# Values of late head pairs on 64 by 32 tiles of TensorE, and two score blocks moved to the other row half

## The chip, the cores and the metric

One Trainium2 chip, of which the kernel uses one core. The metric is device time in microseconds (us) of one launch; 1 us is 1000 ns. A difference under 0.2% (1.76 us) can't be told from no change here.

## What is computed

Sliding-window attention over 8 batches x 8 heads x 576 positions x 64 dims, plain in the first four heads and with dilation 4 in the others, and then a feed-forward layer on the concatenated heads:

```python
scores = q @ k.T / sqrt(64)           # 64 heads in all; a query sees the 32 keys up to its own
attn   = softmax(where(mask, scores, -1e9))
x      = (attn @ v) as 4608 tokens x 512
h      = x @ w_in                     # 512 -> 2048
g      = where(h >= 1, h, where(h <= -1, 0, (h + 1)**2 / 4))
out    = g @ w_out                    # 2048 -> 512
```

## The kernel before

**The feed-forward part** fills most of the time. It goes over 9 blocks of 512 tokens x 16 blocks of 128 hidden units, 144 steps. A step's `layer1` (L515) is 12 matmuls of 128x128 weights against 512 columns, `layer2` (L556) is 12 more, for the step two before. Activations and weights are split into a high and a low part, so each product is three matmuls.

**The attention** is laid between these steps. Heads go in 32 pairs `n`; of a pair, head j=0 has its queries and keys in partitions 0 to 63 and head j=1 in partitions 64 to 127 (the two *row halves* of TensorE). Dilated heads are stored by residue class, so every head is a band: a block of 32 queries needs 64 keys. There are 18 blocks `b` to a head.

Pairs 0 to 3 are early pairs with code of their own. For the others, the late pairs 4 to 31:

- `scores(n)` makes 36 matmuls (L227), one for each block and head: 64 contraction rows, 32 query columns as weights, 64 keys streamed. Each is on a 64 by 32 *tile* of TensorE, that is one row half and one of four column groups `g`; 8 tiles exist. `late_place` says which column group and which place `u` a block takes. Four rounds visit the 8 tiles in turn, and a fifth has the 4 matmuls left. Blocks 8 and 9 have u=4, the *rest* place: both heads share one 128x64 result there, j=0 in partitions 0 to 63, j=1 in 64 to 127.
- `masks` adds the mask table on VectorE (L266, L274, L281), the softmax runs on VectorE, ScalarE and GpSimd, `transpose` (L340) turns the probabilities into `pts`.
- `late_values(n)` makes 20 matmuls (L400) that add into the cleared tile `o`: five key blocks x two key halves (the row half) x two heads, 64 weight columns (the head dims), and 96, 64 or 32 queries streamed. They are on 64 by 64 tiles, of which there are 4. Key half 0 writes the first PSUM bank of `att`, half 1 the second.

`visit_step` (L588) does one attention *visit*: values of pair n, then scores of pair n+1, then the DMA issue of q and k for pair n+2. It runs between `layer1` and `layer2` of every fourth step, for n from 8 to 31; pair 31 has no scores after it. In a visit the j=0 scores go to a spare bank, j=1's to the second bank of `att`, and the rest place to the first bank of `att`. For pairs 4 to 7 a hand-written order (`FIRST`) has steps `V4`..`V7` and `S4`..`S8`, where values and scores stand apart, with feed-forward work between. There the two heads' rest results are in two banks, and `masks` takes two 64-partition operations for them (L281).

Every fp32 matmul shows in the trace as two *passes*: weight load, matmul, weight load, matmul. So 20 matmuls are 40 passes and 36 are 72. The matmuls of the feed-forward part have one pass each.

The order of all engines but the DMA completion is fixed by the order of the calls (a manual schedule).

Of the kernel before, what the change touches and what calls it, by code (L numbers as in the profile page):

```python
# [6 lines left out]
F32 = mybir.dt.float32  # L7
# [4 lines left out]
ALU = mybir.AluOpType  # L12
AX = mybir.AxisListType

B, H, S, D = 8, 8, 576, 64
DM, DF = 512, 2048
WIN, DIL = 32, 4
QB, NB = 32, S // 32
KW = 64
KPAD = S + 32  # L20
# [8 lines left out]
EARLY = 4  # L29
# [37 lines left out]
def body(ctx, tc, qk, v_early, v, mask, mask4, w_in, w_out, out):  # L67
    nc = tc.nc
# [3 lines left out]
    pool = ctx.enter_context(tc.tile_pool(name="pool", bufs=1))  # L72
# [8 lines left out]
    def bank(i, name):  # L81
        return ps.tile([128, TOK], F32, tag=f"b{i}", name=name)

    def banks_of(which, name):
        if which is None:
            both = ps.tile([128, 2, TOK], F32, tag="att", name=name)
            return both, [both[:, 0], both[:, 1]]
        return None, [bank(i, f"{name}_{i}") for i in which]
# [3 lines left out]
    heads, tables = {}, {}  # L92
# [21 lines left out]
    def load_qk(n):  # L114
        hd = heads.setdefault(n, {})
        if "qk" not in hd:
            hd["qk"] = pool.tile([128, 1216], F32, tag="qk", name=f"qk{n}")[:, :S + KPAD]
        hd["q"], hd["k"] = hd["qk"][:, :S], hd["qk"][:, S:]
        nc.sync.dma_start(out=hd["qk"], in_=qk[n])

    def load_v(n, queue=nc.sync):
        hd = heads.setdefault(n, {})
# [34 lines left out]
    def late_place(j, b):  # L157

        half, m, odd = b >= 10, b // 2, b % 2
        if half:  # L160
            return 3 - odd, 5 * j + m - 5
        if m < 4:
            return odd, 5 * j + m
        return (odd if j == 0 else 3 - odd), 4
# [36 lines left out]
                skip_group_check=True,  # L201
            )

    def scores(n, banks=None, at=None):
        if n < EARLY:
            return early_scores(n)
        hd = heads[n]
        cc = pool.tile([128, 704], F32, tag="c", name=f"c{n}", bufs=2)
        hd["cc"] = cc
        hd["c"] = cc[:, :576].rearrange("p (u x) -> p u x", x=KW)  # L210
        hd["st"] = cc[:, 576:603].rearrange("p (s u) -> p s u", s=3)
        if at is None:
            both, (one, two) = banks_of(banks, f"s{n}")
            hd["s"] = both, one[:, : 4 * KW], two[:, : 4 * KW], one[:, 4 * KW : 5 * KW], two[:, 4 * KW : 5 * KW]
        else:
            hd["s"] = None, *at
        todo = {}
        for j in range(2):
            for b in range(NB):
                todo.setdefault(late_place(j, b)[0] + 4 * j, []).append((j, b))  # L220
        for i in range(5):
            for tile in range(8):
                for j, b in todo[tile][i : i + 1]:
                    g, u = late_place(j, b)
                    src = hd["s"][1 + j] if u != 4 else hd["s"][3 + j]
                    r = slice(64 * j, 64 * j + 64)
                    PE.matmul(  # L227
                        out=src[QB * g : QB * g + QB, KW * (u % 5 % 4) : KW * (u % 5 % 4) + KW],
                        lhsT=hd["q"][r, QB * b : QB * b + QB],
                        rhs=hd["k"][r, QB * b : QB * b + KW],  # L230
                        start=True,
                        stop=True,
                    )
# [23 lines left out]
    def by_head(cc):  # L257

        return cc[:, : 10 * KW].rearrange("p (j x) -> p j x", j=2)

    def masks(n, only=None):
        both, *src = heads[n]["s"]
        c, m = heads[n]["c"], msk[:, n % 4 // 2]
        rest = m[:, : 4 * KW].rearrange("p (u x) -> p u x", x=KW)
        if both is not None:
            nc.vector.tensor_tensor(  # L266
                out=by_head(heads[n]["cc"])[:, :, : 4 * KW],
                in0=both[:, :, : 4 * KW],
                in1=m[:, : 4 * KW].unsqueeze(1).broadcast_to([128, 2, 4 * KW]),
                op=ALU.add,  # L270
            )
        for j in range(2) if both is None else ():
            if only in (None, j):
                nc.vector.tensor_tensor(  # L274
                    out=c[:, 5 * j : 5 * j + 4], in0=src[j].rearrange("p (u x) -> p u x", x=KW), in1=rest, op=ALU.add
                )
        if only in (None, 2):
            apart = src[2] is not src[3]
            for j in range(1 + apart):
                r = slice(64 * j, 64 * j + 64) if apart else slice(0, 128)  # L280
                nc.vector.tensor_tensor(out=c[r, 4], in0=src[2 + j][r], in1=m[r, 4 * KW :], op=ALU.add)  # L281

    def spread(n, s):
        st = heads[n]["st"]
# [104 lines left out]
        hd["o"] = list(pieces(n, both, ops))  # L389

    def late_values(n):
        hd = heads[n]
        att, at = hd.pop("at")
        for i in range(5):
            for half in range(2):
                m = 4 * half + i
                a, z = (64, 96) if (half, i) == (1, 0) else (0, 64 if i == 4 else 96)
                r = slice(64 * half, 64 * half + 64)
                for j in range(2):
                    PE.matmul(  # L400
                        out=at[64 * j : 64 * j + 64, 64 * m + a : 64 * m + z],
                        lhsT=hd["v"][r, j, i],
                        rhs=pts[r, 5 * j + i, a:z],
                        start=False,
                        stop=True,
                        skip_group_check=True,
                    )
        hd["o"] = list(joint_pieces(n, at))
        return att

    def joint_pieces(n, at):
        b, c = divmod(n, 4)
        tok0 = b * S
        end = TOK - tok0 % TOK
        step = 1 if c < 2 else DIL
        cuts = sorted({0, min(end, S), S})
        for a, z in zip(cuts, cuts[1:]):
            t, off = divmod(tok0 + a, TOK)
            src, here = at[:, a:z], slice(off, off + z - a)
            if step == 1:  # L420
                yield src, t, c, lambda x, here=here: x[:, here]
            else:
                src = at.rearrange("p (r i) -> p i r", r=DIL)[:, a // DIL : z // DIL]
                yield src, t, c, lambda x, here=here: x[:, here].rearrange("p (i r) -> p i r", r=DIL)
# [161 lines left out]


    def visit_step(s, n):  # L588
        att = late_values(n)
        if n + 1 < NP:  # L590
            spare = bank(4 + s % 2, f"s{n}")
            rest = att[:, 0, :KW]
            scores(n + 1, at=[spare[:, : 4 * KW], att[:, 1, 4 * KW :], rest, rest])
        if n + 2 < NP:
            load_qk(n + 2)
        if n + 1 < NP and n % 2:
            load_v(n + 1)
# [37 lines left out]
    def small_step(count):  # L635
# [14 lines left out]
            out=tables[int(i)], in_=mask4[:, 320 * int(i) : 320 + 384 * int(i)]  # L650
# [51 lines left out]
    for n in range(8, NP):  # L702
        s = 4 * (n - 4) - 2
# [113 lines left out]
```

## Time and profile before

| | |
|---|---|
| median of 3 runs | 878.5 us (878.21 to 878.94) |
| profiled execution | 879.35 us, of which the span is 877.5 us |
| TensorE busy | 869.2 us, 99% of the span |
| TensorE clock granted | full (0.999 on average) |
| VectorE, ScalarE, GpSimd busy | 63%, 35%, 13% |
| mean DMA rate | 66 GB/s |

The profile is one execution. Its timeline view merges neighbouring instructions of one group into a row. A TensorE matmul's shown length runs from when it is taken up to when its last result is written, so matmuls that follow one another overlap in it; the pace is read from the starts. Weight loads are a row of their own (PEld).

### The profile page before, as it was taken

To read this page: it belongs to the slowest core of one execution; us is meant where nothing else is said; L and a number is where in the kernel's file an instruction comes from. 1 tells how busy PE (TensorE), PEld (TensorE's weight loads), DVE (VectorE), ACT (ScalarE), POOL (GpSimd) and SP (SyncE) were. 2 spreads that over 40 slices of the span, in tenths; PEclk is the share of its full clock that TensorE was granted. 3 is DMA by queue.
4 is the path that set the end of the run, shared out by engine and by line. 5 is a ranking of instruction groups with operands and counts; after the bars stand their busy time and mean duration, and the time that the engine had idled before them with its cause. 6 is when DMAs were issued, how large, how long until landed. Compare 5 with 4: busy or idle time off the path is not lost.

```text
span 877.5 us, 16764 instructions
## 1 busy us (share of the span) xinstructions
PE 869.2 (99%) x7138; PEld 712.7 (81%) x7138; DVE 555.6 (63%) x1083; ACT 309.7 (35%) x520; POOL 109.7 (13%) x81
## 2 busy tenths in 40 slices
PE   9999999999999999999999999999999999999998
PEld 7777888888888888888888888888888888888886
DVE  6898887666766676666666666667666443334332
ACT  3988633233333333323323232323332222222222
POOL 2355531110010111111111011011111000000000
PEclk9999999999999999999999999999999999999999
DMA  9981012101210021101210121102110010001001
GB/s 353 415 330 58 30 58 77 60 28 59 76 58 30 4 92 40 59 28 59 78 58 29 59 77 45 36 7 86 50 58 2 1 49 1 0 1 49 1 0 49
DMA packets 17354, 58.12 MB, mean 66 GB/s; under 512 B 1920, under 2 KB 2432, under 8 KB 15232
## 3 DMA queue, kind: packets, MB, share of 16 engines
q1 hardware_dynamic: 17280, 57.06, 18.0%
q8 instruction: 56, 0.92, 0.4%
q14 instruction: 18, 0.15, 0.1%
HBM read 47.61 MB, written 9.44 MB: 65 GB/s over the span
## 4 chain that ended last, share of the span: by engine, by line
PE 92%; ACT 4%; DVE 4%; issue 1%; ACTq 0%; DVEq 0%
PE acc L556 42%; PE h L515 42%; PE o L400 3%; PE s L227 2%; DVE pts L340 1%; PE o L227 1%; DVE m_wi L486 1%; DVE h L535 1%; DVE gl L547 1%; PE s L244 0%; ACT m_wi L473 0%; ACT y L531 0%; PE fill L138 0%; DVE y L525 0%; ACT gh L542 0%
## 5 line engine op out<-in xcount | busy, mean ns | idle before, releaser
L556 PE MATMUL acc<-wo,gh 128*128 128x512 f32 x1152 | 381.8, 392 | 0.1
L515 PE MATMUL h<-xh,wi 128*128 128x512 f32 x1152 | 357.6, 390 | 0.6 <-DVE gl L547 0.5
L556 PEld LDWEIGHTS acc<-wo,gh 128*128 128x128 f32 x1152 | 216.4, 188 | 47.0 <-ACT gh L542 0.5
L515 PEld LDWEIGHTS h<-xh,wi 128*128 128x128 f32 x1152 | 216.2, 188 | 46.3 <-DVE gl L547 1.1
L531 ACT ACTIVATE y<-y,small 128x512 f32<-128x512 f32 x144 | 104.2, 723 | 367.0 <-DVE y L525 366.9
L556 PE MATMUL acc<-wo,gl 128*128 128x512 f32 x576 | 224.8, 390 | 0.3 <-DVE gl L547 0.2
L515 PE MATMUL h<-xl,wi 128*128 128x512 f32 x576 | 224.4, 390 | 0.0
L525 DVE TENSOR_SCALAR y<-h 128x512 f32<-128x512 f32 x144 | 99.4, 690 | 148.5 <-PE h L515 147.5
L535 DVE TENSOR_TENSOR h<-h,y 128x512 f32<-128x512 f32 x144 | 100.7, 700 | 77.5 <-ACT y L531 77.2
L547 DVE TENSOR_TENSOR gl<-h,gh 128x512 fp32r<-128x512 f32 x144 | 99.4, 691 | 69.4 <-ACT gh L542 69.3
L340 DVE STREAM_TRANSPOSE pts<-c 32x256 f32<-32x256 f32 (+2 forms) x336 | 123.1, 366 | 5.7
L556 PEld LDWEIGHTS acc<-wo,gl 128*128 128x128 f32 x576 | 108.2, 188 | 22.6 <-DVE gl L547 1.0
L515 PEld LDWEIGHTS h<-xl,wi 128*128 128x128 f32 x576 | 108.2, 188 | 22.3
L542 ACT CAST gh<-h 128x512 fp32r<-128x512 f32 x144 | 84.4, 586 | 106.8 <-DVE h L535 106.1
L299 POOL TENSOR_TENSOR c<-c 128x576 f32<-128x576 f32 x28 | 32.3, 1154 | 407.7 <-DVE c L291 407.6
L321 POOL TENSOR_TENSOR c<-c 128x576 f32<-128x576 f32 x30 | 35.5, 1183 | 109.4 <-DVE c L317 109.4
L303 ACT ACTIVATE c<-c 128x576 f32<-128x576 f32 x30 | 20.6, 685 | 74.4 <-POOL c L299 64.0
L400 PEld LDWEIGHTS o<-pts,v 64*64 64x64 f32 x1120 | 24.4, 133 | 10.1 <-issue 9.9
L400 PE MATMUL o<-pts,v 64*64 64x96 f32 (+2 forms) x1120 | 28.4, 241 | 0.1
L371 DVE TENSOR_TENSOR xl<-o,xh 128x128 fp32r<-128x128 f32 (+7 forms) x68 | 26.5, 431 | 2.1 <-ACT xh L367 2.1
L367 ACT CAST xh<-o 128x64 fp32r<-128x64 f32 (+9 forms) x68 | 23.3, 398 | 2.7 <-PE o L400 2.6
L227 PE MATMUL s<-qk 64*32 64x64 f32 x1096 | 23.1, 224 | 0.5 <-issue 0.5
(100 smaller groups left out, 369.4 us busy)
## 6 DMA issues: line engine op xcount, KB each, us to landing
qk<-qk_in SPq DMA_DIRECT2D x29, 592.0 KB, 4.0
v<-v_in SPq DMA_DIRECT2D x28, 320.0 KB, 4.5
raw_wi<-w_in SPq DMA_DIRECT2D x8, 1024.0 KB, 13.0
raw_wo<-w_in SPq DMA_DIRECT2D x8, 1024.0 KB, 14.7
out<-out SPq DMA_DIRECT2D x32, 256.0 KB, 2.4
wi_first<-qk_in SPq DMA_DIRECT2D x2, 592.0 KB, 7.7
wo_first<-v_early_in SPq DMA_DIRECT2D x2, 384.0 KB, 11.1
out<-outs SPq DMA_DIRECT2D x3, 256.0 KB, 2.0
```

The source lines that it names most:

```text
L227: PE.matmul(out=src[QB * g : QB * g + QB, KW * (u % 5 % 4) : KW * (u % 5 % 4) + KW], lhsT=hd["q"][r, QB * b : QB * b + QB], rhs=hd["k"][r, ...
L299: nc.gpsimd.tensor_tensor(out=c, in0=c, in1=spread(n, 0), op=ALU.subtract)
L321: engine.tensor_tensor(out=c, in0=c, in1=spread(n, 2), op=ALU.mult)
L340: nc.vector.transpose(out=to, in_=c)
L400: PE.matmul(out=at[64 * j : 64 * j + 64, 64 * m + a : 64 * m + z], lhsT=hd["v"][r, j, i], rhs=pts[r, 5 * j + i, a:z], start=False, stop=Tr ...
L515: PE.matmul(out=hp, lhsT=weight("wi", f, w, slice(128 * c, 128 * c + 128)), rhs=xtile(t)[x][:, c], start=start and (c, w, x) == terms[0], ...
L525: nc.vector.tensor_scalar(out=gs[t, f][0], in0=hps[t, f], scalar1=-1.0, scalar2=1.0, op0=ALU.max, op1=ALU.min)
L531: nc.scalar.activation(out=y, in_=y, func=AF.Square, bias=half_t, scale=0.5)
L535: nc.vector.tensor_tensor(out=hp, in0=hp, in1=gs[t, f][0], op=ALU.max)
L542: nc.scalar.copy(out=g_tile("gh", t, f), in_=hps[t, f])
L547: nc.vector.tensor_tensor(out=g_tile("gl", t, f), in0=hp, in1=gh.bitcast(F32), op=ALU.subtract)
L556: PE.matmul(out=acc[m], lhsT=g[:, 128 * m : 128 * m + 128], rhs=weight("wo", f, w, slice(0, DM)), start=f == 0 and i == 0, stop=f == NF - ...
```

## The change

It does three things. The values of a late pair are cut in their weight columns: each of the 20 matmuls with 64 head dims becomes two with 32 (`part` 0 to 3 instead of j 0 to 1), on the same 64 by 32 tiles as the scores. Of the scores, blocks 8 and 9 of head j=1 (u=4) take their queries and keys from partitions 0 to 63, from a second copy of these (`again`) that the host appends to q and k; so the rest place is written by one row half only. The load of q and k of a late pair is 1344 columns instead of 1184. Where the rest results were in two banks they are now in one, and `masks` needs one operation for them. `late_values` becomes a generator `value_rounds` that `late_values` runs to its end; `scores` has an argument `rounds` that no caller gives, so values still stand wholly ahead of scores.

```diff
     def load_qk(n):
...
-            hd["qk"] = pool.tile([128, 1216], F32, tag="qk", name=f"qk{n}")[:, :S + KPAD]
-        hd["q"], hd["k"] = hd["qk"][:, :S], hd["qk"][:, S:]
-        nc.sync.dma_start(out=hd["qk"], in_=qk[n])
+            hd["qk"] = pool.tile([128, 1344], F32, tag="qk", name=f"qk{n}")
+        w = S + KPAD + (160 if n >= EARLY else 0)
+        hd["q"], hd["k"], hd["again"] = hd["qk"][:, :S], hd["qk"][:, S:], hd["qk"][:, S + KPAD :]
+        nc.sync.dma_start(out=hd["qk"][:, :w], in_=qk[n][:, :w])
...
-    def scores(n, banks=None, at=None):
+    def scores(n, banks=None, at=None, rounds=None):
...
-                todo.setdefault(late_place(j, b)[0] + 4 * j, []).append((j, b))
+                g, u = late_place(j, b)
+                todo.setdefault(g if j == 0 or u == 4 else g + 4, []).append((j, b))
         for i in range(5):
+            if rounds is not None:
+                next(rounds, None)
             for tile in range(8):
                 for j, b in todo[tile][i : i + 1]:
                     g, u = late_place(j, b)
-                    src = hd["s"][1 + j] if u != 4 else hd["s"][3 + j]
-                    r = slice(64 * j, 64 * j + 64)
+                    if j and u == 4:
+                        r, at_q, at_k = slice(0, 64), hd["again"][:, QB * (b - 8) :], hd["again"][:, QB * (b - 6) :]
+                    else:
+                        r, at_q, at_k = slice(64 * j, 64 * j + 64), hd["q"][:, QB * b :], hd["k"][:, QB * b :]
+                    src = hd["s"][1 + j] if u != 4 else hd["s"][3]
...
         if only in (None, 2):
-            apart = src[2] is not src[3]
-            for j in range(1 + apart):
-                r = slice(64 * j, 64 * j + 64) if apart else slice(0, 128)
-                nc.vector.tensor_tensor(out=c[r, 4], in0=src[2 + j][r], in1=m[r, 4 * KW :], op=ALU.add)
+            nc.vector.tensor_tensor(out=c[:, 4], in0=src[2], in1=m[:, 4 * KW :], op=ALU.add)
...
     def late_values(n):
+        rounds = value_rounds(n)
+        for _ in rounds:
+            pass
+
+    def value_rounds(n):
...
-                for j in range(2):
+                for part in range(4):
+                    x = slice(QB * (part % 2), QB * (part % 2) + QB)
+                    j = part // 2
                     PE.matmul(
-                        out=at[64 * j : 64 * j + 64, 64 * m + a : 64 * m + z],
-                        lhsT=hd["v"][r, j, i],
+                        out=at[QB * part : QB * part + QB, 64 * m + a : 64 * m + z],
+                        lhsT=hd["v"][r, j, i, x],
                         rhs=pts[r, 5 * j + i, a:z],
...
+            yield
```

TensorE's order in a visit, before (a row is line, result tile, operands, partitions x columns of the result, count; `o` is the bank pair `att`, `s` the spare bank):

```order
L400 MATMUL o_1590<-pts,v_1525 64x96 [waits DVE_49,DMAHW4_49,PE_49,Activation_49]
L400 MATMUL o_1590<-pts,v_1525 64x96
L400 MATMUL o_1590<-pts,v_1525 64x32 [waits DVE_49]
L400 MATMUL o_1590<-pts,v_1525 64x32
L400 MATMUL o_1590<-pts,v_1525 64x96 x12
L400 MATMUL o_1590<-pts,v_1525 64x64 x4
L227 MATMUL s_1690<-qk_1528 32x64 [waits DMAHW6_49]
L227 MATMUL s_1690<-qk_1528 32x64 x3
```

The same place with the change:

```order
L412 MATMUL o_1665<-pts,v_1600 32x96 [waits DVE_49,DMAHW4_49,PE_49,Activation_49]
L412 MATMUL o_1665<-pts,v_1600 32x96 x3
L412 MATMUL o_1665<-pts,v_1600 32x32 [waits DVE_49]
L412 MATMUL o_1665<-pts,v_1600 32x32 x3
L412 MATMUL o_1665<-pts,v_1600 32x96 x24
L412 MATMUL o_1665<-pts,v_1600 32x64 x8
L234 MATMUL s_1785<-qk_1603 32x64 [waits DMAHW6_49]
L234 MATMUL s_1785<-qk_1603 32x64 x3
```

The counts of the values double, all on half the columns; the waits, and the scores' place behind the last value, stay.

VectorE's order around `mask4`, before (`s` is the score tile, `c` the masked scores):

```order
L266 TENSOR_TENSOR c_555<-s_556,small 128x2x256
L281 TENSOR_TENSOR c_555<-s_556,small 64x64 x2
```

The same place with the change:

```order
L273 TENSOR_TENSOR c_555<-s_556,small 128x2x256
L285 TENSOR_TENSOR c_555<-s_556,small 128x64
```

One operation less, here and in `mask5` to `mask8`.

## Rows read from the trace of the kernel before

**Rows 1.** The page: busy share of each engine, and the chain that ended last.

```profile
PE 869.2 (99%) x7138; PEld 712.7 (81%) x7138; DVE 555.6 (63%) x1083; ACT 309.7 (35%) x520; POOL 109.7 (13%) x81
PE 92%; ACT 4%; DVE 4%; issue 1%; ACTq 0%; DVEq 0%
```

**Rows 2.** Timeline, TensorE, one visit: start us, us, engine, line, operation, tiles, form, count.

```profile
303.24 0.62 PE L515 MATMUL h<-xh,wi 128*128 128x512 f32 x2
303.69 0.39 PE L515 MATMUL h<-xl,wi 128*128 128x512 f32 x1
304.01 0.99 PE L400 MATMUL o<-pts,v 64*64 64x96 f32 x40
304.93 0.26 PE L227 MATMUL s<-qk 64*32 64x64 f32 x4
...
305.01 0.24 PE L227 MATMUL s<-qk 64*32 64x64 f32 x4
...
305.07 0.24 PE L227 MATMUL s<-qk 64*32 64x64 f32 x4
...
305.13 0.24 PE L227 MATMUL s<-qk 64*32 64x64 f32 x4
...
305.52 0.39 PE L227 MATMUL o<-qk 64*32 64x64 f32 x12
305.83 0.50 PE L556 MATMUL acc<-wo,gh 128*128 128x512 f32 x1
```

**Rows 3.** Timeline of short windows of that visit: single passes, and weight loads.

```profile
304.01 0.29 PE L400 MATMUL o<-pts,v 64*64 64x96 f32 x1
304.79 0.22 PE L400 MATMUL o<-pts,v 64*64 64x64 f32 x1
304.93 0.24 PE L227 MATMUL s<-qk 64*32 64x64 f32 x1
305.01 0.22 PE L227 MATMUL s<-qk 64*32 64x64 f32 x1
305.26 0.15 PEld L227 LDWEIGHTS s<-qk 64*32 64x32 f32 x5
305.34 0.22 PE L227 MATMUL s<-qk 64*32 64x64 f32 x1
305.59 0.15 PEld L227 LDWEIGHTS o<-qk 64*32 64x32 f32 x4
```

**Rows 4.** Groups by line and form: count | busy us, mean ns | idle before.

```profile
L227 PE MATMUL o<-qk 64*32 64x64 f32 x920 | 21.7, 224 | 0.0
```

**Rows 5.** Lines L400 and L227 in that visit: durations min/median/max, first and last start.

```profile
L400 PE MATMUL o<-pts,v x40: 215/243/294, 304.0 to 304.8; 64*64 64x96 f32 x28, 64*64 64x64 f32 x8, 64*64 64x32 f32 x4
...
L227 PEldq EVENT_SEMAPHORE  x1: 51/51/51, 304.4 to 304.4; - x1
```

**Rows 6.** S4: line L227's semaphore instruction, and the timeline of its weight loads.

```profile
L227 PEldq EVENT_SEMAPHORE  x1: 1903/1903/1903, 31.5 to 31.5; - x1
...
33.39 0.83 PEld L227 LDWEIGHTS s<-qk 64*32 64x32 f32 x72 [0.90 <-PE h L515]
```

**Rows 7.** Timeline around values without scores behind them: V31, V5, V4.

```profile
684.95 0.99 PE L400 MATMUL o<-pts,v 64*64 64x96 f32 x40
685.87 0.50 PE L556 MATMUL acc<-wo,gh 128*128 128x512 f32 x1
...
78.97 0.50 PE L515 MATMUL h<-xh,wi 128*128 128x512 f32 x1 [0.46 <-DVE gl L547]
...
55.44 0.20 PEld L400 LDWEIGHTS o<-pts,v 64*64 64x64 f32 x6 [0.20 <-DVE pts L340]
```

**Rows 8.** Line L281: durations min/median/max, first and last start.

```profile
L281 DVE TENSOR_TENSOR c<-o,small x23: 214/215/216, 141.4 to 665.2; 128x64 f32<-128x64 f32 x23
L281 DVE TENSOR_TENSOR c<-s,small x10: 205/216/229, 35.0 to 110.0; 64x64 f32<-64x64 f32 x10
```

**Rows 9.** DMA issues: count, KB each, us to landing.

```profile
qk<-qk_in SPq DMA_DIRECT2D x29, 592.0 KB, 4.0
```

## What the change will do: the prediction

> **What bounds the kernel now.** I read the page first. TensorE is busy for 99% of the span and makes 92% of the chain that ended last [rows 1]. So a nanosecond more or less on TensorE is a nanosecond of the time, unless TensorE was about to wait for something else anyway. The change is a matter of TensorE's time inside the attention visits.
>
> Next I read the timeline of TensorE through one visit [rows 2], and short windows of it [rows 3]. There are 23 visits with values and scores: line L227 has 920 passes into `o`, 40 to a visit [rows 4]. The reader should see four things in the visit.
>
> First, a pause at each change of tile shape. The last value pass starts at 304.79 and streams 64 columns. Such a pass holds its tile for 56 ns: the score rows for the same tiles start at 305.01 and 305.07 [rows 2]. So the values are done streaming near 304.84, and the first score pass starts at 304.93: some 91 ns in which TensorE does nothing. The other changes look the same: the last `layer1` matmul starts at 303.69 and such matmuls go at 0.225 us (303.24 to 303.69 is two), so it streams to some 303.92, and the values start at 304.01. The last score row ends at 305.91, so its last pass of 0.22 starts near 305.69, streams to 305.75, and `layer2` starts at 305.83.
>
> Second, the values run at the pace of their columns. Each of four tiles has ten passes; 96 columns take 56 x 96/64 = some 82 ns, so 8 x 82 + 2 x 56 = 770 ns, and the rows say 304.01 to 304.79 (774 ns by the single starts).
>
> Third, the scores do not. Their first 32 passes, 16 matmuls, start within 0.25 us. The 18th matmul loads its weights only at 305.26 [rows 3], although the first tiles are free again from 305.13 + 0.056 = 305.19. The first matmul's second pass started at 305.01 and ended 0.22 later, at 305.23. So the 18th comes 30 ns after the first has *ended*. From there on one matmul enters about every 17 ns: the 15 first passes behind the 18th's reach to 305.52. Then the 35th's load stands at 305.59, while the 18th's second pass ended at 305.34 + 0.22 = 305.56: again 30 ns. I read this as a **limit of 17 unfinished fp32 matmuls**. One turn of these 17 places for scores lasts 24 (weights that were not loaded ahead; the first pass is longer by that, 0.24 against 0.22) + 56 (first pass) + 217 (second pass to its end) + 31 = 328 ns. It gives the scores' length: the 35th at 2 x 328 = 656, the 36th 17 later, its second pass 80 (24 + 56) later: 753 ns. Measured: 304.93 to 305.69, 0.76.
>
> Fourth, the limit holds for values too. A separate semaphore instruction (it waits for the load of q and k) stands between the 20th value and the first score. It ran at 304.4 [rows 5], 0.4 us after the first value, whose two passes end at about 304.01 + 0.05 + 0.08 + 0.24 = 304.38. It could not pass the values earlier. With 20 matmuls on four tiles this costs nothing, as 17 places are more than the tiles take in.
>
> **The change part by part.**
>
> *Values, 40 matmuls instead of 20.* Each of the eight tiles has the same ten passes with the same columns as each of the four before, so by streaming alone it stays 774 ns. But now 23 of the 40 must wait for a place. A turn with 96 columns is 24 + 82 + 243 (the median length of a value pass [rows 5]) + 31 = 380 ns. The 18th enters at 380, the 35th at 760, the 40th at 760 + 5 x 17 = 845, and its second pass starts at 925. So the values take **925 instead of 774 ns**. [...]
>
> *No change of shape between values and scores.* The 91 ns go, with the 24 ns of first weights, and the scores enter behind the 40th value as places come free. The one thing between is the semaphore instruction. It takes 51 ns [rows 5]; before, it ran under the values at no cost, now it stands in a stream in which entering is the limit. At S4 one waited 1.903 us from 31.5, to 33.4, and the first load stands at 33.39 [rows 6]: behind its end nothing more is lost that the rows could show. Bounds: 0, if it is absorbed, and 75, if the 24 ns of a fresh weight load come on top. I take the 51 ns of its own row.
>
> Now the sum, from the first value: the first score enters at 845 + 17 + 51 = 913, the 11th at 1083. The 12th needs the 35th value's place: 760 + 328 = 1088 (that value has 64 columns), so 17 after the 11th, 1100. The 18th score needs the first one's place: 913 + 328 = 1241. The 29th needs the 12th's: 1428. The 35th needs the 18th's: 1569. The 36th is at 1586, and its second pass starts at 1666. Before, by the same rule, it was 920 + 753 = 1673. **Difference: -7 ns a visit, -0.2 us over 23 visits.** Without the semaphore's 51 ns the same steps end at 1615, -58 ns or -1.3 us; with 75 at 1690, +17 ns or +0.4 us.
>
> *Values without scores behind them.* V4 to V7 and V31 keep both changes of shape and only get longer, by 925 - 774 = 151 ns each. V31 pays it in full: `layer2` follows without a wait [rows 7]. V5 pays nothing: behind it TensorE waits 0.46 us for VectorE's `gl`. V4 already waits in its middle for transposes. I take V31 and V7 in full and half of V4 and V6: +0.45 us, between 0.15 and 0.75.
>
> *Masks of pairs 4 to 8.* Five operations of 216 ns leave VectorE [rows 8]; the one left is 128x64, for which the visits show 215. At most this is worth 1.1 us, at least nothing. TensorE feels VectorE only at a few short waits in this stretch, like the 0.20 and 0.46 us in rows 7. I take -0.2.
>
> *Two blocks in the other row half.* Rounds one to four still have eight tiles and round five four matmuls; the limit counts matmuls, not tiles. Nothing.
>
> *Longer q and k.* A load goes from 592 to 672 KB, its landing from 4.0 [rows 9] to, in proportion, an estimated 4.5 us. It is issued right behind the scores and needed a visit later; visits stand 23.8 us apart (304.01 to V31's 684.95 is 16 of them [rows 2, 7]). Covered; if one early load were not, +0.5 us.
>
> *Sum:* -0.2 + 0.45 - 0.2 = about +0.1 us on the profiled 879.35 us (span 877.5 and 1.85 around it), thus on the median, which stands 0.85 lower, **878.6 us**. All lower bounds together give -2.3, all upper ones +1.65.
>
> **The rivals.**
>
> *B, the limit does not bind the values.* The narrow matmuls may free their places sooner. Then values keep 774 ns, the scores enter at 774 + 56 = 830 and take their 753: 1583, -90 ns a visit, -2.1 us; V4 to V7 and V31 cost nothing; with the masks -2.3: **876.2 us**. For it speaks that the limit never cost the values anything in this trace, so I have it from the scores and from one semaphore. Against it, that the same form of matmul, 64x32, showed it. [...]
>
> *C, slower: scores can't enter while values run.* The pause may come not from the shape but from the first score's wait for its inputs, or from the hand-over of the PSUM banks of `att`, which both write. Then values last 925, the pause of 91 stays, and the scores start at 925 + 56 + 91 = 1072 instead of 920: +152 ns, +3.5 us, and with the other terms **882.2 us**. It decides as soon as scores are held until the values have drained. Against it: all three pauses stand at changes of shape and are equally long, and the 3rd value matmul, which waits for a semaphore too, shows no pause. [...]
>
> **How the numbers follow.** I give my forecast 0.70, B 0.18, C 0.12. A measurement can tell 0.2%, 1.76 us. The forecast lies within that but for its outermost bounds: 0.65 same, 0.03 faster, 0.02 slower. B is 2.3 below the median, mostly faster: 0.17, and 0.01 same. C is slower: 0.12. So faster 0.20, same 0.66, slower 0.14. The range goes from B with half a microsecond to spare, 875.6, to the forecast's upper bounds and the first part of C, 880.5; C's full price is left out.
>
> **What the profile of the changed kernel would show.** The values of a visit from first to last start: 925 ns means the limit is right, 774 means B. Between last value and first score: passes that follow within some 70 ns, the semaphore's mark among them, mean the pause is gone; 150 ns mean C. First value to last score pass: 1.67 us as before. The semaphore instruction some 0.85 us after the first value instead of 0.4. V31 longer by 0.15 us. L285 with 28 operations instead of 33. The prediction is wrong if the visit as a whole changes by more than 75 ns.

## The result and the profile after

The change made the kernel slower: 883.0 us (median of 5 runs, 881.9 to 885.1) against 878.5; ratio 1.0054, with a 95% interval of 1.0039 to 1.0069. The runs of the kernel before, five here too, lie within 0.7 us, those of the changed one within 3.2. The profiled execution took 883.68 us with a span of 881.2, 3.7 more than before. The spans of the five runs go from 880.1 to 881.6 us; what a run takes outside its span is 1.7 to 3.5 us in them, and 1.7 to 1.9 in all but one of the other runs on record. So only 1.5 of the 3.2 us of scatter lie in the program itself; where the rest comes from stays open.

The page of the changed kernel, next to [rows 1] and [rows 9]:

```profile
PE 870.1 (99%) x8258; PEld 714.1 (81%) x8258; DVE 554.0 (63%) x1078; ACT 309.6 (35%) x520; POOL 109.9 (12%) x81
q8 instruction: 64, 1.05, 0.5%
PE 91%; ACT 3%; DVE 2%; DMA 2%; issue 1%; SPq 1%; ACTq 0%; DVEq 0%
qk<-qk_in SPq DMA_DIRECT2D x28, 672.0 KB, 4.4
```

TensorE has 1120 more matmul passes and is busy for 0.9 us longer; the rest of the 3.7 us is time in which it does nothing. The second row has no place in the prediction: the DMA queue that the page calls `instruction` (packets, MB, share). Of the kernel before it reads:

```profile
q8 instruction: 56, 0.92, 0.4%
```

TensorE's timeline with the change: an ordinary visit, the one at 304, the end of the next, and V31 (line L412 is the values, L234 the scores, L567 `layer2`):

```profile
161.06 1.15 PE L412 MATMUL o<-pts,v 64*32 64x96 f32 x80
...
162.90 0.50 PE L567 MATMUL acc<-wo,gh 128*128 128x512 f32 x1
...
304.12 1.14 PE L412 MATMUL o<-pts,v 64*32 64x96 f32 x80
...
305.64 0.39 PE L234 MATMUL o<-qk 64*32 64x64 f32 x12
307.76 0.39 PE L567 MATMUL acc<-wo,gh 128*128 128x512 f32 x1 [1.73 <-ACT xh L371]
...
334.36 0.39 PE L567 MATMUL acc<-wo,gl 128*128 128x512 f32 x1 [0.99 <-issue]
...
688.39 1.15 PE L412 MATMUL o<-pts,v 64*32 64x96 f32 x80
689.47 0.50 PE L567 MATMUL acc<-wo,gh 128*128 128x512 f32 x1
```

An ordinary visit lasts 162.90 - 161.06 = 1.84 us from the first value to `layer2`; before it was 305.83 - 304.01 = 1.82 [rows 2]. So the visits themselves are nearly what they were. V31 is longer, 1.08 against 0.92 us [rows 7]. But the visit at 304.12 ends in a hole. The row of 334.36 is the end of another. The weight loads show how the two holes look from inside:

```profile
305.96 0.19 PEld L567 LDWEIGHTS acc<-wo,gh 128*128 128x128 f32 x1
307.76 0.19 PEld L567 LDWEIGHTS acc<-wo,gl 128*128 128x128 f32 x1 [1.62 <-issue]
...
332.99 0.19 PEld L567 LDWEIGHTS acc<-wo,gl 128*128 128x128 f32 x1
334.37 0.41 PEld L567 LDWEIGHTS acc<-wo,gh 128*128 128x128 f32 x2 [1.19 <-issue]
```

A matmul's weights are loaded at 305.96, and the matmul itself starts 1.80 us later; at 332.99 again, 1.37 us later. Between the load and its matmul stands no semaphore. The releaser that the view names for the first (ACT, `xh`) is thus a chance neighbour; the second is honest with "issue", waiting for nothing that is shown. A third, small one lies inside the scores of the visit before, 0.12 us. Together 3.3 us, from a weight load to its matmul. But a load stands some 0.2 us ahead of its matmul in any case (the one at 332.76 does), so what the holes cost is read from the visits' starts. Here are the first visit before (`L400`), the first visit with the change, and the visits around the holes:

```profile
137.36 0.99 PE L400 MATMUL o<-pts,v 64*64 64x96 f32 x40
```
```profile
137.29 1.09 PE L412 MATMUL o<-pts,v 64*32 64x96 f32 x76
...
280.16 1.15 PE L412 MATMUL o<-pts,v 64*32 64x96 f32 x80
...
329.65 1.15 PE L412 MATMUL o<-pts,v 64*32 64x96 f32 x80
...
354.65 1.15 PE L412 MATMUL o<-pts,v 64*32 64x96 f32 x80
```

Between the first visit and V31's [rows 7] the changed kernel takes 551.1 us instead of 547.6. Of these 3.5 us 3.0 are in the three intervals that hold the holes (280.16 to 354.65), and the other twenty give -0.04 to 0.10 us each.

**Theory 1: TensorE's instructions run out.** By the trace an fp32 matmul is four instructions (two weight loads, two matmuls), one of the feed-forward part two. Before, TensorE executed 2 x 7138 of them and some 70 semaphore instructions, and 56 packets came on that queue, 0.92 MB, so 16.4 KB each: 256 instructions to a load (14346 against 56 x 256 = 14336). Counted from the trace, the three holes stand behind 6593, 7105 and 7617 executed instructions: 512 and 512 apart, two loads exactly. I read it so: TensorE executes one load while the next is moved, and stands still where it comes to the *border* between two loads before the next is there. That is the theory; the trace shows the counts and the transfers, not what starts a transfer. In the feed-forward part 256 instructions last 128 x 0.227 = 29 us, and behind V31, where nothing else is left, six transfers in a row start 28.9 to 29.3 us apart (697.70 to 842.82), 254 to 258 executed instructions from one to the next. A visit now has 76 matmuls, 304 instructions, in 1.84 us; before it had 56, 224, less than a load. By the theory, if a border falls into the first part of a visit, the next border is reached before its load is there. In the visit of 304.12 the load was moved at 305.33:

```profile
DMA  0000000000000900000000000000000000000000
...
q8 instruction: 1, 0.02, 7.3%
```

That is the DMA view of the stretch from 305 to 306, forty slices of 25 ns. The matmul comes at 307.76, 2.4 us behind the start of this transfer; at the second hole it is 2.4 us again, and in all holes of over 0.3 us in the visits of all traces here 2.2 to 3.0 us. From visit to visit there are 498 instructions, 14 short of two loads, so the border moves on by 14 places in each, and only few visits have it in the bad part: the border of the three holes falls behind the 35th, 49th and 63rd instruction of the visit (its *place*), and the hole stands one load of 256 further on.

**Rival:** the holes belong to those visits, to their data, the longer load or the shared bank.

### The profile page after: what moved, and what is told of

Read it like the earlier page. It is cut to its first block, busy times and chain, and to the rows that moved or that the text cites. A ratio compares the mean times of both kernels' runs of the same rounds, so it can differ in the third digit from the quotient of the medians.

```text
span 881.2 us, 18999 instructions
## 1 busy us (share of the span) xinstructions
PE 870.1 (99%) x8258; PEld 714.1 (81%) x8258; DVE 554.0 (63%) x1078; ACT 309.6 (35%) x520; POOL 109.9 (12%) x81
## 4 chain that ended last, share of the span: by engine, by line
PE 91%; ACT 3%; DVE 2%; DMA 2%; issue 1%; SPq 1%; ACTq 0%; DVEq 0%
PE acc L567 43%; PE h L526 42%; PE o L412 3%; DMA v<-v_early_in 2%; PE o L234 1%; PE s L234 1%; DVE pts L344 1%; DVE m_wi L497 1%; ACT wi L504 0%; ACT y L542 0%; DVE h L546 0%; PE o L386 0%; ACT raw_wi L491 0%; ACT m_wi L484 0%; DVE gl L558 0%
## 5 line engine op out<-in xcount | busy, mean ns | idle before, releaser
L567 PE MATMUL acc<-wo,gh 128*128 128x512 f32 x1152 | 381.4, 392 | 1.7 <-ACT xh L371 1.7
L567 PEld LDWEIGHTS acc<-wo,gh 128*128 128x128 f32 x1152 | 216.2, 188 | 48.5 <-issue 1.2
L567 PE MATMUL acc<-wo,gl 128*128 128x512 f32 x576 | 224.7, 390 | 1.2 <-issue 1.0
L567 PEld LDWEIGHTS acc<-wo,gl 128*128 128x128 f32 x576 | 108.2, 188 | 23.9 <-issue 1.6
L412 PEld LDWEIGHTS o<-pts,v 64*32 64x32 f32 x2240 | 27.6, 105 | 10.1 <-issue 9.9
L412 PE MATMUL o<-pts,v 64*32 64x96 f32 (+2 forms) x2240 | 32.3, 238 | 0.0
L234 PE MATMUL s<-qk 64*32 64x64 f32 x1096 | 22.9, 224 | 0.5 <-issue 0.5
```

The costliest lines, as they stand in the source:

```text
L234: PE.matmul(out=src[QB * g : QB * g + QB, KW * (u % 5 % 4) : KW * (u % 5 % 4) + KW], lhsT=at_q[r, :QB], rhs=at_k[r, :KW], start=True, stop ...
L412: PE.matmul(out=at[QB * part : QB * part + QB, 64 * m + a : 64 * m + z], lhsT=hd["v"][r, j, i, x], rhs=pts[r, 5 * j + i, a:z], start=False ...
L567: PE.matmul(out=acc[m], lhsT=g[:, 128 * m : 128 * m + 128], rhs=weight("wo", f, w, slice(0, DM)), start=f == 0 and i == 0, stop=f == NF - ...
```

## The experiments

Ten runs. Where a run has several rounds its ratio is to the kernel before on the same chip; a run without a ratio is one profiled execution. The cuts of code are against the changed kernel unless said otherwise, and `...` marks what is left out.

### The values back on 64 by 64 tiles

```diff
-                for part in range(4):
-                    x = slice(QB * (part % 2), QB * (part % 2) + QB)
-                    j = part // 2
+                for j in range(2):
                     PE.matmul(
-                        out=at[QB * part : QB * part + QB, 64 * m + a : 64 * m + z],
-                        lhsT=hd["v"][r, j, i, x],
+                        out=at[64 * j : 64 * j + 64, 64 * m + a : 64 * m + z],
+                        lhsT=hd["v"][r, j, i],
```

> The change with one part undone: the values of late pairs are 20 matmuls on 64 by 64 tiles again; the longer q and k, the two blocks in the other row half and the single mask operation stay. Theory 1 (TensorE's instructions run out: 76 fp32 matmuls of 4 instructions in a visit are 304, more than one load of 256): a visit now has 224, none of the three stalls of 0.1 to 1.8 us is left, the visits last what they lasted before, and the time is 878.4 us (878.0 to 878.8), the same as before. Rival (the stalls come from the other parts of the change, the longer load or the shared bank of the rest place): at least two stalls stay, near 306 and 333 us, and the time is 881.5 or more.

Measured: 877.7 us, ratio 0.9987 (0.9979 to 0.9996). No hole, and 56 instruction loads as before; the visit at 302.73 lasts 1.82 us up to `layer2` (L565):

```profile
302.73 0.99 PE L410 MATMUL o<-pts,v 64*64 64x96 f32 x40
...
304.55 0.50 PE L565 MATMUL acc<-wo,gh 128*128 128x512 f32 x1
```

The rest of the change costs nothing; the narrow values alone make it slow. That it is even faster than before was not expected by the theory; below.

### The border moved

```diff
-tab0 qk0 small52 fill2.5 fill1.5 pm0 S0 max0 max0.1 sub0 pm1 tab1 qk1 S1 max1.0 sub0.1 exp0 max1.2
+tab0 qk0 small36 fill3.5 fill1.5 pm0 S0 max0 max0.1 sub0 pm1 tab1 qk1 S1 max1.0 sub0.1 exp0 max1.2
```

> The whole change, with 16 of the 52 warm-up matmuls at the start left out (64 instructions fewer; a wider filler matmul beside them keeps the start's length). Nothing in the visits differs. Theory 1: each border between two loads of 256 instructions now lies 64 instructions later in the program, which is where it lay about 4.6 visits later before. The stalls leave the visits at 279.8, 303.8 and 329.3 us and come in those near 184.6 and 208.4, perhaps 232 us; they again end at executed counts of 193 modulo 256, and together make 2.5 to 4 us, so the time is 883 us (882 to 884.5). Rival (the stalls belong to the work of those visits, the results of the values read by ScalarE or the transfers of that time): they stay at 279.8, 303.8 and 329.3 us.

Measured: 886.9 us, above the range expected. The holes left their visits and came in those of 185 and 213 us:

```profile
186.83 0.31 PE L234 MATMUL o<-qk 64*32 64x64 f32 x9
188.94 0.30 PE L234 MATMUL o<-qk 64*32 64x64 f32 x3 [1.80 <-issue]
189.17 0.50 PE L567 MATMUL acc<-wo,gh 128*128 128x512 f32 x1
...
190.47 1.05 PE L567 MATMUL acc<-wo,gh 128*128 128x512 f32 x2
191.32 0.63 PE L567 MATMUL acc<-wo,gl 128*128 128x512 f32 x1
```

The place is theory 1's, the rival falls. The time is not: I had overlooked two things. The border comes round again after 256 / 14 = 18 visits, which gave two more holes, in the visits of 619 and 644 us. And behind the long one the matmuls start every 0.43 us (190.47 to 191.32 is two) instead of 0.23: the clock granted from 190.5 to 193.4 us was 0.50, half of the full one; see the run with the border held badly.

### The border held in place, well and badly

Cutting a first-layer matmul in two adds two instructions, for 16 ns as measured below. With seven cuts in every fourth step, and one more semaphore instruction that the trace shows there, the period is 498 + 14 + 1 = 513, two loads and one.

```diff
-        for c, w, x in terms:
-            PE.matmul(
-                out=hp,
+        for k, (c, w, x) in enumerate(terms):
+            cut = i % 4 == 0 and 18 < i < 110 and 0 < k <= 7
+            for z in (slice(0, 256), slice(256, 512)) if cut else (slice(0, 512),):
+                PE.matmul(
+                    out=hp[:, z],
...
-                rhs=xtile(t)[x][:, c],
+                    rhs=xtile(t)[x][:, c, z],
...
```

> The whole change, and in one step of the feed-forward part in every four, seven of the twelve matmuls of the first layer are cut in two of 256 columns: 161 matmuls, so 322 instructions, more than the change has. From one visit to the next there are then 513 instructions instead of 498, nearly two loads of 256, so the border falls in all visits where it fell in the first one, behind about the 207th of the 304 instructions. Theory 1: no visit has a stall, although TensorE has more to do: 883.0 less 3.2 for the stalls, plus 161 cuts at 0 to 20 ns, 5 taken: 880.6 us (879.8 to 883). Rival (the stalls belong to the work of those visits): they stay, and the time is 883.8 us or more.

The second kernel has, in addition, `small28 fill4.5` in place of `small52 fill2.5`.

> The same with 24 of the 52 warm-up matmuls left out (96 instructions fewer, a wider filler matmul in their place), so that the border falls near the 47th instruction in all visits, as it did in the one with the longest stall. Theory 1: nearly each of the 23 visits ends in a stall of 1.0 to 1.9 us: 880.6 plus some 35 us, 915 us (900 to 925). Rival: two or three stalls as before, 884 us.

Measured: 882.8 us (ratio 1.0044, 1.0029 to 1.0059) and 906.7 us. The two differ in where the border lies and in nothing else of the visits. With the border behind place 184 to 206 there is no hole in any visit (one of 0.5 us stands far ahead of the cuts, in S5); the visits stand 23.93 us apart against 23.82, so a cut costs 0.11 / 7 = 16 ns, more than the 5 that I took, a guess that came from no run. That eats what the holes gave back: by its time alone this run could not be told from the changed kernel, and it is the trace without holes that speaks for theory 1. With the border behind places 46 to 25, these are TensorE's waits in the scores (line, what was waited for, us, times, longest), and the holes of the first visit (place 46) and the sixth (place 42):

```profile
PE o L234 <- issue: 13.1, 13, 2.0
```
```profile
142.94 0.21 PE L234 MATMUL o<-qk 64*32 64x64 f32 x1 [2.03 <-issue]
...
276.49 0.30 PE L234 MATMUL o<-qk 64*32 64x64 f32 x3 [0.38 <-issue]
```

By place the holes are (from one matmul's start to the next): 2.0 to 2.2 us at places 46 to 43 (five visits), 0.4 to 1.0 us at 42 to 34 (none at 37), 0 to 0.2 us at 33 to 31, nothing at 30 to 25 (the period of 513 moves the border back by one in each visit). So 915 was too much, as the border left the bad part halfway. Three of the five holes of 2 us cost some 1.6 us more than their length. The windows view ahead of the second of the five and behind it (us; busy and count of PE, PEld, DVE, ACT, POOL; granted clock; DMA):

```profile
160.00:164.00 4.00, 4.00 (x20) 3.30 (x19) 2.32 (x5) 1.31 (x2) 0.00 (x0) 1.00 0.00 0
168.20:170.00 1.80, 1.10 (x4) 0.85 (x5) 0.78 (x2) 0.72 (x3) 0.00 (x0) 0.78 0.00 0
170.00:172.00 2.00, 2.00 (x6) 1.61 (x5) 1.95 (x5) 0.00 (x0) 0.60 (x1) 0.50 0.91 290
```

Behind 2 us without a matmul the granted clock fell to 0.50; from 172 to 174 us it was 0.85 on average. The changed kernel's spans scatter by 1.5 us; that holes vary in length, and that a long one can nearly double its price, would explain it, but those runs have no trace.

### As many instructions without the change

The cut is against the kernel before.

```diff
-        for i in range(5):
+        turns = [0, 1, 2, 3, 4] if at is None else [0, 1, 2, 3, 4, 0, 1, 4]
+        for i in turns:
```

> The kernel before, without any part of the change, and 20 of the 36 scores of a visit are computed a second time into the same place: 76 matmuls, so 304 instructions in a visit as with the change, but all tiles, loads and masks as before. Theory 1: stalls come where the borders of 256 instructions lie as in the run with 16 warm-up matmuls fewer: in the third and fourth visit (near 185 and 209 us) and in the third and second from last (near 625 and 650 us), 3 to 6.5 us in all. The 20 scores themselves cost a turn of 328 ns and three steps of 17 ns, 0.38 us a visit. Time 878.6 + 23 x 0.38 + 4.7 = 892 us (890 to 894.5). Rival (the stalls need the narrow values, the longer load or the shared bank): no stall, 887.4 us.

Measured: 895.3 us, 0.8 above the range expected. The holes are where the theory put them (1.9 us at 188.5, 0.6 in the next visit, then 0.4 and 0.8 us in the visits of 627 and 652), though no part of the change is in this kernel:

```profile
188.50 0.34 PE L228 MATMUL o<-qk 64*32 64x64 f32 x10
190.50 0.30 PE L228 MATMUL o<-qk 64*32 64x64 f32 x3 [1.66 <-issue]
```

With the 1.6 us that the clock takes they make 5.4; the twenty scores cost 0.42 us a visit (24.23 instead of 23.81) where 0.38 was expected, and S4 came 0.9 us later than before. The rival's 887.4 us is out of reach.

### Two visits of the 23 with wide values

```diff
+                cols = 64 if n in (14, 27) else 32
+                for part in range(128 // cols):
+                    y = slice(cols * part, cols * part + cols)
+                    j, x = part // (64 // cols), slice(cols * part % 64, cols * part % 64 + cols)
...
```

> The whole change, but in two visits of the 23, those of pairs 14 and 27, the values stay on 64 by 64 tiles (20 matmuls). Pair 14 is where the first stall stands; its 80 instructions fewer move the border in all later visits by 80 places, past the places at which the second and third stall stood, and pair 27 is the next that would be reached. Theory 1: all three stalls go at no cost: 883.0 - 3.3 = 879.8 us (879.2 to 880.6), with visits of 2.73 us as with the change. Rival (the stalls belong to their visits): those of pairs 15 and 16, at 304 and 329 us, stay, 882.9 us.

Measured: 880.2 us, ratio 1.0015 (1.0006 to 1.0024). All three holes are gone, at 304 and 329 us too, in visits that have not changed:

```profile
304.96 1.14 PE L413 MATMUL o<-pts,v 64*32 64x96 f32 x80
...
306.82 0.50 PE L568 MATMUL acc<-wo,gh 128*128 128x512 f32 x1
```

Against the changed kernel's 1.0054 this is 0.0039 of 878.5, so 3.4 us for the holes, with some 1.5 either way by the two intervals. By the traces it is less: from the first visit to V31's it is 548.4 us instead of 551.1, so 2.7, next to the 3.0 above.

```profile
138.18 1.09 PE L413 MATMUL o<-pts,v 64*32 64x96 f32 x76
...
686.57 1.14 PE L413 MATMUL o<-pts,v 64*32 64x96 f32 x80
```

### The first score ahead of the values

```diff
-        late_values(n)
-        att = heads[n]["att"]
+        att = heads[n]["at"][0]
...
-            scores(n + 1, at=[spare[:, : 4 * KW], att[:, 1, 4 * KW :], rest])
+            scores(n + 1, at=[spare[:, : 4 * KW], att[:, 1, 4 * KW :], rest], behind_first=lambda: late_values(n))
```

(`scores` calls `behind_first` once, behind its first matmul.)

> The whole change, and the first score of a visit, which waits for the load of q and k, is issued ahead of the values instead of behind them; nothing is added. Theory 1 says two things of a visit: that the semaphore instruction between values and scores costs some 70 to 84 ns, since it stands in a stream in which entering is the limit, so values and scores together last 1.62 us instead of 1.69; and that the stalls stay in the visits at 280, 304 and 329 us, since the count of instructions is the same. Time 881.4 us (880.5 to 883.5, by the length of the stalls). Rival (the semaphore costs nothing, the gap of 84 ns is the limit itself): 1.69 us as with the change.

Measured: 885.8 us, a miss in both parts. From the first matmul to the last score 1.72 us instead of 1.69 (by the single starts): the semaphore's gap is gone, but the values now last 1.03 us, 100 ns more, because the score takes the tile of the first value. And there are six holes, in the visits from 233 to 332 us and at 667: the bad part of a visit has grown to places 2 to 62. The semaphore instruction of the values suggests why. With the change, for the visit of 232.52 (line L412), and with the score ahead, for the visit of 233.27 (L415):

```profile
L412 PEldq EVENT_SEMAPHORE  x1: 51/51/51, 228.4 to 228.4; - x1
```
```profile
L415 PEldq EVENT_SEMAPHORE  x1: 51/51/51, 231.7 to 231.7; - x1
```
```profile
230.95 0.69 DVE L561 TENSOR_TENSOR gl<-h,gh 128x512 fp32r<-128x512 f32 x1 [0.71 <-ACT gh L556]
```

TensorE's sequencer passed it 4.1 us ahead of the visit; now it comes at 231.7, right behind the end of `gl` at 231.64, and is only 1.6 us ahead. I take it that the first score waits for `gl` to free the spare bank that it writes, and holds the sequencer. If a load is asked for when the sequencer comes to a border, which no trace shows, a shorter lead would bring it later, closer to where it is needed. That the lead is the cause was not tried by itself.

> A version that could beat both: narrow values only in the visits, with the first score ahead of them; values on 64 by 64 tiles for pairs 4 to 7 and 31, which have no scores behind them, and for pairs 10 and 22, where the border of 256 instructions would make a stall. Theory 1: no stall, and 21 visits of 1.62 us from first value to last score instead of the 1.67 us of the kernel with the values back on 64 by 64 tiles (877.7 us): 877.7 - 21 x 0.045 = 876.8 us (876.0 to 877.6). Rival (the score ahead waits for its load or its bank and holds the values): 877.7 us or more.

This kernel takes both edits, with wide values, and no score ahead, for n in (4, 5, 6, 7, 10, 22, 31). Measured: 881.9 us (1.0036, 1.0023 to 1.0049): it has the same 1.71 us, and holes of 0.2 to 0.8 us in four visits, at places 6 to 28. A miss.

The next kernel is this one with two edits: the order of the tiles, and pairs 8 and 19 in place of 10 and 22.

```diff
-            for tile in range(8):
+            for tile in (7, 0, 1, 2, 3, 4, 5, 6):
...
```

> The narrow values with the first score ahead once more, as in the version that was to beat both, but that first score is one on the tile which the values reach last of the eight (row half 1, column group 3), where it stood on the tile of the first value before; and the visits with values on 64 by 64 tiles are now those of pairs 8 and 19 (besides 4 to 7 and 31), chosen so that no border of 256 instructions falls behind the first 65 of a visit, as the score ahead had made stalls there too. Theory (the score ahead cost 100 ns in the values because it delayed their first tile, and without that the missing semaphore instruction gives its 84 ns): 1.62 to 1.65 us from the first matmul of a visit to its last score, no stall, 876.9 us (876.2 to 877.6). Rival (any tile that gets a 41st matmul is late by its two passes, whichever it is): 1.71 us a visit, 878.5 us or more.

Measured: 878.1 us, ratio 0.9994 (0.9985 to 1.0002). No hole, and the visit is 1.61 us by the single starts: 82 ns less than with the change, as the theory wanted. But it didn't become time, and 878.1 is above the range expected. The visits stand as far apart as with wide values (next run): 302.91 to 326.69 is 23.78 us, and there 302.79 to 326.57 is the same.

```profile
302.91 0.24 PE L234 MATMUL o<-qk 64*32 64x64 f32 x1
...
304.67 0.50 PE L571 MATMUL acc<-wo,gh 128*128 128x512 f32 x1
305.00 0.40 PE L571 MATMUL acc<-wo,gl 128*128 128x512 f32 x1
305.25 0.40 PE L571 MATMUL acc<-wo,gh 128*128 128x512 f32 x1
...
326.69 0.24 PE L234 MATMUL o<-qk 64*32 64x64 f32 x1
```

Its first ten matmuls behind a visit start every 0.23 to 0.24 us instead of 0.227 (305.00 to 305.25), 67 ns in all. What slows them stays open.

### Two mask operations again

This edit stands on top of the values back on 64 by 64 tiles.

```diff
-            nc.vector.tensor_tensor(out=c[:, 4], in0=src[2], in1=m[:, 4 * KW :], op=ALU.add)
+            for r in (slice(0, 64), slice(64, 128)) if n < 9 else (slice(0, 128),):
+                nc.vector.tensor_tensor(out=c[r, 4], in0=src[2][r], in1=m[r, 4 * KW :], op=ALU.add)
```

> The run with the values back on 64 by 64 tiles, which came out 1.0 us faster than the kernel before, and in it the one mask operation of pairs 4 to 8 for the rest place is two operations on 64 partitions again. Theory (VectorE's five operations of 216 ns were on the path): 878.5 us, the time of the kernel before. Rival (they were covered, and the microsecond comes from elsewhere, most likely from the start, ahead of the first late pair, where runs of one kernel differ by as much): 877.6 us (877.3 to 877.9).

Measured: 878.1 us, ratio 0.9994 (0.9985 to 1.0003), between the two theories. By the profiles the single operation is worth little: from the first S4 score to the first value of the first visit it is 103.92 us with two operations and 103.78 with one, one execution each. The microsecond of the first experiment lies ahead of S4. The first row is the kernel with the values back, its S4 at 32.30; before, S4's weights were loaded at 33.39 [rows 6]; the second row is the run with two wide visits, 34.80:

```profile
32.30 0.96 PE L234 MATMUL s<-qk 64*32 64x64 f32 x72 [0.51 <-issue]
```
```profile
34.80 0.29 PE L234 MATMUL s<-qk 64*32 64x64 f32 x8 [0.51 <-issue]
```

Up to there all these programs give TensorE the same instructions; even the kernel before and the one with more scores, whose starts are alike in all, came to 33.4 and 34.3. Whether a program has its own start or it is chance was not tried, and with one profile of each kernel it is not shown either that runs of one kernel differ there, as was expected above; it makes differences of a microsecond between two of these kernels unsafe.

## Why the prediction was wrong

The forecast was 878.6 us, with 0.14 for slower; the time of 883.0 lies outside the range of 875.6 to 880.5.

*The step that failed* is the frame of the sum: "So a nanosecond more or less on TensorE is a nanosecond of the time, unless TensorE was about to wait for something else anyway. The change is a matter of TensorE's time inside the attention visits." I counted passes, places and tiles, and left out that 20 more fp32 matmuls are 80 more instructions that have to be brought in. 304 instead of 224 in a visit passes the 256 of one load; some 3 us of the 4.5 come from that alone (3.0 by the changed kernel's intervals, 2.7 and 3.4 by the trace and the time of the kernel with two wide visits), as shown by taking the narrow values away, by moving the border, by holding it at a good and at a bad place, and by adding as many instructions to the kernel before. It was in neither of the rivals, though the row of the instruction queue stands on the page.

The counts show 256 instructions to a load. Behind V31 in the changed kernel, at 29 us to a load, no matmul starts more than 0.228 us behind the one before it, so nothing is lost there. In a visit 304 go in 1.84 us, and the matmul behind a hole of over 0.3 us started 2.2 to 3.0 us behind the start of its load's transfer.

*The limit of 17 unfinished matmuls:* its times are right; that there are 17 places is my reading of them, and nothing shows the places themselves. The ends of matmuls that it counts from are borne out by those who wait for them: in the changed kernel VectorE's `y` starts never less than 37 ns, and in three of four steps 37 to 39, behind the shown end of the last `layer1` matmul. The values last 0.93 us from first to last start (V31: 1.08 - 0.92 = 0.16 us longer, forecast 0.15). The 18th enters at 383 ns (380 forecast), the 35th at 764 (760), the first score at 918 (913), the 18th score at 1248 (1241), all from the visit of 304.12 by the single weight loads. Rival B is out.

*The pause of 91 ns between values and scores:* gone, as forecast; the first score starts 17 ns after the last value pass. Rival C is out. That its 882.2 us came near the measured 883.0 is chance: what came instead is no pause between values and scores.

*The semaphore instruction:* it ran 0.84 us after the first value (0.85 forecast), and took its 51 ns:

```profile
L234 PEldq EVENT_SEMAPHORE  x1: 51/51/51, 305.0 to 305.0; - x1
```

Without it, and with one score out of the way, the run with the other tile was 82 ns shorter; less that score's 17, the semaphore costs 65, within the bounds of 0 to 75 and above the 51 taken. *The visit as a whole* was forecast at -7 ns and came out at +15 to +20, at the upper edge of the bounds of -58 and +17: the last two scores enter 10 and 26 ns later than counted.

*Values without scores behind them:* V31 +0.16 us as forecast. V4 to V7, 0.30 us of the 0.45 forecast, cost nothing that shows: from S4 to the first visit the changed kernel needs 103.5 us against 103.9 before. *Masks:* worth 0.14 us by the profiles, 0.2 forecast, within what a run can't tell. *Longer q and k:* covered; the landing is 4.4 us against 4.5 forecast. *The whole:* of the 3.7 us between the two spans 3.0 are in the intervals with holes, 0.5 in the other visits, 0.16 in V31, 0.4 ahead of S4, and -0.4 between S4 and the first visit. What the medians' 4.5 has beyond that is not in the profile; about half a microsecond of it is time outside the spans.

## What to carry to other kernels

Count instructions as well as time: where a stretch runs more than one instruction load (here 256; an fp32 matmul is four) in less time than the next load takes to arrive (here 2.2 to 3.0 us from the start of its transfer on), the engine can come to stand still. Whether it does depends on where the border happens to fall, so an edit far ahead can switch it on or off (16 warm-up matmuls fewer took the holes from 280 to 334 us away and made others from 188 us on). It shows as a wait for "issue", or for a chance neighbour, between a weight load and its own matmul; here 80 instructions fewer in each of the two visits that the border would reach took it away. The denser stream of small matmuls was not worth its instructions here: by streaming alone it saved nothing.

## What the runs showed that I had not expected

- A hole of 2 us in TensorE's work can bring the granted clock down to 0.50 and cost some 1.6 us more. Its length does not decide it: of the eight holes in all traces with 1.88 to 2.24 us from start to start, five brought the clock down, the one of 1.88 among them, and three did not: that of the changed kernel at 305.8 (1.95) and two of 2.2.
- How much of a visit is safe seems to hang on the lead of TensorE's sequencer: with 4.1 us of lead a border up to place 30 made no hole, with 1.6 us one at place 2 did. In the badly held kernel the holes jump from 0.6 to 2.2 us between places 42 and 43, and the transfers jump with them: the load's packet starts 1.0 to 1.5 us behind the visit's first matmul at places 46 to 43, and between 0.3 us ahead of it and level with it at 42 to 38. At which moment the engine asks for a load stays open.
- A single score on the tile of the first value cost the values 100 ns (1.03 us from first to last start against 0.93); on the tile that they reach last it cost nothing (302.92 to some 303.84 us, 0.92).
- No version beat the kernel before by more than 0.2%: the values back on wide tiles came nearest, with 0.13%.
